# A fused attention and Fourier-mixing kernel: one batch's turn moved from DMA to TensorE, and the loads and scores around it reordered

## The chip, the cores and the metric

The kernel runs on one core of a Trainium2 chip. The metric is the device time of one execution in microseconds (us): 305.38 us before the change, the median of three runs (304.95 to 306.23). The profiled run has a span of 303.7 us from its first to its last instruction, at a mean granted TensorE clock of 0.994.

## The reference

Two models are chained. In the first, a sequence x of 512 tokens and a state of 32 rows attend to each other, for 8 batches and 8 heads of 64 columns:

```
scores  = x @ state^T / 8;   a  = softmax(scores);   xread = a  @ state
scores2 = state @ x^T / 8;   a2 = softmax(scores2);  sread = a2 @ x
u0 = concat(xread, sread)            # 544 rows of 512 columns per batch
```

In the second, the 544 x 512 result of each batch is mixed by a Fourier transform over rows and columns, normalised, and passed through a two-layer network:

```
u  = u0 + real(fft(fft(u0, rows), columns))
un = (u - mean) / sqrt(var + 1e-6)
out = u + relu(un @ w_ch1) @ w_ch2   # 512 -> 2048 -> 512
```

The matrix products run in bf16 with sums in float32.

## The kernel before

**Stages of one batch.** `attend(b)` turns the batch's x (512 x 512, in the bf16 tile `xin`) and its state block into `xT` and `sT`, so that columns of heads lie on partitions. Two `scores` steps multiply them (PSUM tile `esp`, L437) and ScalarE takes the exponential (tile `E`, L442); for batches from 2 on, `turn_scores` turns E on TensorE (tile `eTp`, L449) and ScalarE copies it to `ET` (L450). `xread` (L462, tiles `xrp` and `xfp`) and `sread_by_head` (L482) read the values; VectorE divides by the sums (L470, L471, L489) into the row tiles XF and XR. `fold` on VectorE (L534 to L549) adds and subtracts mirrored rows and columns, so that the transform needs only a quarter of the products; `read_low`, `fold_low` and `fold_low_again` do the same for 32 "low" rows on GpSimd (L519 to L531).

`transform(b)` does the Fourier transform as two sets of matmuls: `over_s` along the rows (L783, PSUM tile `gp`, copied to G by ScalarE, L784), `over_d` along the columns (L679 and L680, tile `yp`). VectorE adds the input (tile U, L684), takes the statistics (L337, L339), and centres (tile `ub`); `turn_u` turns the result into `unT`, on TensorE (L851, with a copy at L852) for batches 0 and 1, by DMA (L847) for the later ones. Two tiny GpSimd instructions per row tile form the inverse deviation (L343, L344; in the first batches these "roots" are collected and issued later).

`layer1(b)` has 16 steps of four 128 x 512 matmuls (L926; for batch 0 quarter steps of 128 columns, L936), each with a relu on ScalarE (L928, L938). `layer2(b)` has 16 steps of four matmuls (L990, tile `po`); each fourth ends with `store`, in which VectorE adds U (tile `ot`, L957) and SyncE stores it. The lists are called L and M for batch 0: M[0] to M[3] are the four quarters of the first row tile, M[4] to M[7] of the second. M[0] and M[4] use the first quarter of the second weights `w2`, M[1] and M[5] the second, and so on.

**What sets the order.** Every engine runs its instructions in the order in which the program records them. The opening and all of batch 0 and 1 up to L1224 are a list written by hand; from batch 1's layers on (L1226 to L1250), `weave` merges streams of steps: a stream is given with two numbers between 0 and 1, the stretch of the round over which its steps are spread.

**Buffers.** The PSUM pools are `psQ` (three tiles, tag q: gp, yp, eTp, tp and others), `psF` (three tiles, tag c: ph, po and the warm-up) and `psX` (one double tile, tag x). `xs`, the float32 landing place of x, has two buffers; `xin` has two as well.

**The names that the change touches.** `x_by_dma` (L355) is the first batch whose x and state are turned by DMA on SyncE's queue (L377 for sT, L388 for xT) and not on TensorE. `turn_all` (L400) turns x and the state of one batch on TensorE, 16 + 4 transposes, and leaves three copies in a list: sT and half of xT on ScalarE, the other half on VectorE. Before, batch 1 alone uses it. `load_x(b)` issues seven DMAs for one batch's x (L145), `turn_in_dram` reverses a batch's state rows from DRAM to DRAM (L155), `load_state` loads them (L113). `second_weights(lo, hi)` issues quarters of w2 on GpSimd's queue (L325); in front of it stands a `gate`, a tiny GpSimd copy that reads x of batch 2 and so holds the weight loads until that x has landed. `cast_columns` casts x of batch 2 to bf16 on GpSimd; the last four columns are cast behind another gate, which reads the last quarter of w2 (L1174), so that the DMA turns of batch 2 start only when the weights have landed:

```
    nc.gpsimd.tensor_copy(gate, w2[:, 12:16, 0])
    cast_columns(508, 512, slice(0, 4))
    turned[2]()
    load_x(3)
```

Of the kernel before, what the change touches and what calls it, by code (L numbers as in the profile page):

```python
# [30 lines left out]
def kernel(  # L31
# [8 lines left out]
    nc = tc.nc  # L40
    B, H, S, D = x.shape
# [67 lines left out]
    def states(lo, hi):  # L109
        return stf[:, lo:hi] if lo < 3 else stl[:, lo - 3:hi - 3]  # L110

    def load_state(lo, hi, src=state):
        nc.sync.dma_start(  # L113
            out=states(lo, hi).rearrange("p b g d -> p (b g) d"),
            in_=src[lo:hi].rearrange("b (g hh) j d -> (hh j) (b g) d", hh=4),
        )

    xin_bufs = [singles.tile([128, 4, 514], BF16, name=f"xin{i}") for i in range(2)]
    xs_of = {}
# [34 lines left out]
    def turn_in_dram(lo, hi):  # L154
        nc.sync.dma_start(out=s_dram[lo:hi].rearrange("b h j d -> (b h) j d"),  # L155
                          in_=state[lo:hi, :, ::-1, :].rearrange("b h j d -> (b h) j d"))
# [19 lines left out]
    gate = singles.tile([128, 4], F32, name="gate")  # L176
# [9 lines left out]
    w2 = singles.tile([128, FC, dm], BF16, name="w2")  # L186
# [136 lines left out]
    def second_weights(lo, hi):  # L323
        for q in range(lo, hi):
            nc.gpsimd.dma_start(out=w2[:, q * 4:(q + 1) * 4, :], in_=w2v[:, q * 4:(q + 1) * 4, :])  # L325
# [3 lines left out]
    def qt(name, dt=F32):  # L329
        return psQ.tile([128, 512 if dt == F32 else 1024], dt, name=name, tag="q")  # L330
# [21 lines left out]
    first_roots = []  # L352


    x_by_dma, u_by_dma = 2, 2  # L355


    turned = {}

    def attend(b):  # L360
# [24 lines left out]
        def turn_x(g):  # L385
            if b >= x_by_dma:
                for si in ((0, 1), (3, 2))[g]:
                    nc.sync.dma_start_transpose(out=xT[:, :, 128 * si:128 * si + 128], in_=xin[:, si, 1:513])  # L388
                return
            p = qt("xTp", BF16)  # L390
            for si in range(2):
                for pr in range(4):
                    o = si * 512 + pr * 128
                    nc.tensor.transpose(p[:, o:o + 128], xin[:, 2 * g + si, 1 + 128 * pr:129 + 128 * pr], ident)
            (nc.vector.tensor_copy if g == (b == 0) else nc.scalar.copy)(
                xT[:, :, 256 * g:256 * g + 256].rearrange("p a (s c) -> p s a c", c=128),
                p.rearrange("p (s a c) -> p s a c", s=2, c=128))
# [15 lines left out]
        copies, pairs = [], []  # L413
# [137 lines left out]
        if b < 2:  # L551
            first = [turn_state, lambda: turn_x(0), lambda: turn_x(1)]
            if b == 1:
                first = [turn_all] + [lambda i=i: copies[i]() for i in range(3)]
            first += [lambda: scores_t(0), lambda: scores_t(1),
                     lambda: scores(0), lambda: scores(1)]
        else:
            first = [lambda: scores(0), lambda: scores(1), lambda: turn_scores(1), lambda: turn_scores(0)]
            if b >= x_by_dma:
                turned[b] = lambda: (b > 2 and turn_state(), turn_x(0), turn_x(1))  # L560
                turned[b, 0] = turn_state
            else:
                first = [turn_state, lambda: turn_x(0), lambda: turn_x(1)] + first
        read = lambda c0, rev, o: lambda: xread(c0, rev, "xrp" if rev else "xfp", o, apart=(b == 0 and not rev))
        if b < 2:
            second = [read_low, fold_low, fold_low_again, read(0, False, XF[:, 0, 0:512]), sread_heads,
# [347 lines left out]
    def layer1(key):  # L914
        low = isinstance(key, tuple)
        n = 128 if low else 512
        hT = wk.tile([128, FC, n], BF16, name="hTL" if low else "hT", tag="hTL" if low else "hT", bufs=1 if low else 2)
        h_of[key] = hT
        per = 512 // n

        def step(i):
            ph = psF.tile([128, 512], F32, name="ph", tag="c")
            for f in range(per * i, per * i + per):
                o = (f % per) * n
                for c in range(DC):
                    nc.tensor.matmul(ph[:, o:o + n], lhsT=w1[:, c, f * 128:(f + 1) * 128], rhs=un_of[key][:, c, :],  # L926
                                     start=(c == 0), stop=(c == DC - 1))
            nc.scalar.activation(hT[:, per * i:per * i + per, :].rearrange("p a b -> p (a b)"), ph, AF.Relu,  # L928
                                 scale=-1.0 / 512 if key == 0 else -1.0 if key in flipped else 1.0)

        def quarter_step(i, r):
            ph = psF.tile([128, 512], F32, name="ph", tag="c")
            for f in range(4 * i, 4 * i + 4):
                o = 128 * (f % 4)
                for c in range(DC):
                    nc.tensor.matmul(ph[:, o:o + 128], lhsT=w1[:, c, f * 128:(f + 1) * 128],  # L936
                                     rhs=un_of[key][:, c, 128 * r:128 * r + 128], start=(c == 0), stop=(c == DC - 1))
            nc.scalar.activation(hT[:, 4 * i:4 * i + 4, 128 * r:128 * r + 128], ph.rearrange("p (a b) -> p a b", b=128),  # L938
                                 AF.Relu, scale=-1.0 / 512 if key == 0 else -1.0 if key in flipped else 1.0)

        if key == 0:
            return [lambda i=i, r=r: quarter_step(i, r) for r in range(4) for i in range(FC // 4)]
        return [lambda i=i: step(i) for i in range(FC // per)]
# [80 lines left out]
    turn_state, turn_x0, score, read, sread, state_rows, even, odd = open_batch()  # L1024
    begin, terms_of, low_of, out_of, keep_low, over_d, add_sums, centre_sums, turn_u, spread, done, keep_middle = transform(0)
# [83 lines left out]
    psF = ctx.enter_context(tc.tile_pool(name="psF", bufs=3, space=bass.MemoryType.PSUM))  # L1109
    pool_of = {"warm": (psF, "c")}  # L1110
    s1, r1 = attend(1)
    scores_next, reads_after = attend(2)
    L, M = layer1(0), layer2(0)
    over_s1, over_d1, add1, centre1, turn_u1, done1 = transform(1)
    turns1, copies1, s1 = s1[0], s1[1:4], s1[4:]
    def cast_columns(lo, hi, i):
        nc.gpsimd.tensor_copy(xin_bufs[0][:, i, 1 + lo:1 + hi], xs_of[2].rearrange("p (i c) -> p i c", i=4)[:, i, lo:hi])
# [13 lines left out]
    nc.gpsimd.tensor_tensor(gate, xs_of[0][:, 0:4], w1[:, :, 3 * 512], op=ALU.add)  # L1131
    load_x(2)
    turn_in_dram(3, 4)
    turned[2, 0]()
    load_state(3, 4, s_dram)
    turn_u(0, 1)
    add_sums(0, 0)
    centre_sums(0, 0)
# [12 lines left out]
    L[2]()  # L1151
    s1[2]()
    r1[0]()
    nc.gpsimd.tensor_copy(gate, xs_of[2].rearrange("p (i c) -> p i c", i=4)[:, :, 0])
    second_weights(0, 2)
    r1[1]()
    r1[2]()
    second_weights(2, 4)
    L[3]()
    s1[3]()  # L1160
    r1[3]()
# [7 lines left out]
    r1[7]()  # L1169
    nc.gpsimd.tensor_copy(gate, XQs[1].rearrange("p (g j c) -> p g j c", g=2, j=4)[:, 1, 3, 0:4])  # L1170
    for i in range(4):
        cast_columns(0, 508, slice(i, i + 1))
    state_blocks(3, 4, nc.gpsimd.tensor_copy)
    nc.gpsimd.tensor_copy(gate, w2[:, 12:16, 0])  # L1174
    cast_columns(508, 512, slice(0, 4))
    turned[2]()
    load_x(3)
    turn_in_dram(4, B)
    L[6]()
    L[7]()  # L1180
    turn_u(1, 0)
    spread(0, 1)
    state_ones(2, B)
    L[8]()
# [29 lines left out]
    turn_u1(1, 1)  # L1214
    M[6]()
    turn_u1(1, 0)
    spread(0, 0)
    spread(1, 1)
    spread(1, 0)
# [5 lines left out]
    l2, scores_first = M, scores_next  # L1225
    for b in range(1, B + 1):  # L1226
        reads_next = reads_after
        l2, l2_now = (layer2(b), [l2[7]] + l2[8:]) if b == 1 else (layer2(b) if b < B else [], l2)
        streams = [(l2_now + (layer2(("L", b // 4)) if b in (3, 7) else []), 0, 1)]
        if b == 1:  # L1230
            streams = [(l2_now[:5], 0, 0.38), (l2_now[5:], 0.6, 1)]
        if b < B:
            streams.append((layer1(b), 0.13 if b == 2 else 0.08, 1))
        if b + 1 < B:
            if b == 1:
                streams.append(([lambda: load_state(4, B, s_dram), lambda: state_blocks(4, B, nc.gpsimd.tensor_copy)], 0.2, 0.95))
                streams.append((scores_first[0:2], 0, 0.08))
                streams.append((scores_first[2:4], 0.08, 0.15))
            streams.append((reads_next, 0.17 if b == 1 else 0, 0.42 if b == 1 else 0.3))
            streams.append((transform(b + 1), 0.58 if b == 1 else 0.47, 0.88 if b == 1 else 0.85))  # L1240
        if b + 2 < B:
            scores_next, reads_after = attend(b + 2)
            streams.append(([lambda: (cast_x(b + 2), turned[b + 2]())], 0.15 if b == 1 else 0.2, 0.2))
            streams.append((scores_next, 0.5, 1))
        if b + 3 < B:
            streams.append(([lambda: load_x(b + 3)], 0.35, 0.35))
        if b in (3, 7):
            streams.append((low_rows(b // 4), 0.02, 0.2))
            streams.append((layer1(("L", b // 4)), 0.36, 0.8))
        weave(*streams)  # L1250
# [30 lines left out]
```

The softmax here doesn't subtract the row's maximum and nothing guards it: scores larger than these inputs give would overflow.

## Time and profile before

| engine | busy us | share of the span |
|---|---|---|
| TensorE, matmuls (PE) | 288.9 | 95% |
| TensorE, weight loads (PEld, beside PE) | 165.3 | 54% |
| VectorE (DVE) | 180.4 | 59% |
| ScalarE (ACT) | 136.3 | 45% |
| GpSimd (POOL) | 92.7 | 31% |

SyncE (SP) issues most DMAs and computes nothing. A busy share is a mean over the whole span; where time can be saved is read from the slices of the span, from the waits of the busiest engine, and from the timeline at those places. In the timeline the columns are the start, the busy time, engine, line, operation and tiles, and in brackets how long the engine had been idle before it and for whom.

Some times that are needed below, all from the trace: TensorE begins the quarter steps of batch 0's first layer at 22.3 us, M[0] at 38.3 and the weave (M[7]) at about 52. Batch 2's x is issued at 21.3 to 28.3 us and batch 3's at 52.1 to 57.2. The four quarters of w2 are issued at 31.5, 32.3, 38.2 and 39.0 us and take 5.4 to 8.3 us to land.

### The profile page before, as it was taken

To read this page: it belongs to the slowest core of one execution; us is meant where nothing else is said; L and a number is where in the kernel's file an instruction comes from. 1 tells how busy PE (TensorE), PEld (TensorE's weight loads), DVE (VectorE), ACT (ScalarE), POOL (GpSimd) and SP (SyncE) were. 2 spreads that over 40 slices of the span, in tenths; PEclk is the share of its full clock that TensorE was granted. 3 is DMA by queue.
4 is the path that set the end of the run, shared out by engine and by line. 5 is a ranking of instruction groups with operands and counts; after the bars stand their busy time and mean duration, and the time that the engine had idled before them with its cause. 6 is when DMAs were issued, how large, how long until landed. Compare 5 with 4: busy or idle time off the path is not lost.

```text
span 303.7 us, 6027 instructions
## 1 busy us (share of the span) xinstructions
PE 288.9 (95%) x2301; PEld 165.3 (54%) x2333; DVE 180.4 (59%) x446; ACT 136.3 (45%) x253; POOL 92.7 (31%) x226
## 2 busy tenths in 40 slices
PE   5999989888999999999999999999999999999995
PEld 5789966434544645456545554455454544555443
DVE  8868987573879385755637575675668474000012
ACT  6887557434633553244533445254524442334200
POOL 6764862750481044301315022702240131000000
PEclk9999999997999999999999999999999999999999
DMA  8998793958533952467433684253243023600355
GB/s 155 197 204 185 129 175 73 209 110 179 113 86 72 207 131 78 107 144 167 96 80 72 148 164 89 69 123 82 74 90 69 37 75 86 133 2 35 87 128 132
DMA packets 110824, 34.86 MB, mean 115 GB/s; under 512 B 101980, under 2 KB 106332, under 8 KB 110796
## 3 DMA queue, kind: packets, MB, share of 16 engines
q1 hardware_dynamic: 100076, 28.72, 43.3%
q0 software_dynamic: 4224, 4.19, 8.6%
q10 hardware_dynamic: 6496, 1.57, 2.5%
q8 instruction: 18, 0.29, 0.4%
q14 instruction: 10, 0.08, 0.1%
HBM read 22.41 MB, written 14.02 MB: 120 GB/s over the span
## 4 chain that ended last, share of the span: by engine, by line
PE 76%; DMA 6%; DVE 5%; POOL 5%; SPq 4%; issue 3%; ACT 1%; POOLq 0%; DVEq 0%
PE po L990 33%; PE ph L926 32%; DMA w<-in_moe_w_ch_dram 2%; PE gp L783 2%; SPq L145 2%; DMA xT<-xin 2%; SPq L388 1%; DMA xs<-in_x_dram 1%; PE po L982 1%; PE esp L437 1%; PE yp L680 1%; PE yp L679 1%; PE xfp L462 1%; DVE U L684 1%; DVE st L337 1%
## 5 line engine op out<-in xcount | busy, mean ns | idle before, releaser
L990 PE MATMUL po<-w,hT 128*128 128x512 bf16 x480 | 122.2, 379 | 1.3 <-issue 0.5
L928 ACT ACTIVATE hT<-ph 128x512 bf16<-128x512 f32 x112 | 66.9, 597 | 121.0 <-PE ph L926 118.9
L926 PE MATMUL ph<-unT,w 128*128 128x512 bf16 x432 | 113.7, 382 | 0.7
L926 PEld LDWEIGHTS <-w 128*128 128x128 bf16 x576 | 50.9, 98 | 47.3 <-issue 1.1
L990 PEld LDWEIGHTS <-hT 128*128 128x128 bf16 x496 | 46.6, 98 | 46.0
L957 DVE SCALAR_TENSOR_TENSOR ot<-po,rstd,U 128x512 f32<-128x512 f32 (+2 forms) x33 | 24.1, 732 | 50.8 <-PE po L990 46.0
L787 POOL COPY GL<-G 128x128 bf16<-128x128 bf16 x7 | 2.0, 289 | 75.7 <-ACT G L784 75.7
L684 DVE TENSOR_TENSOR U<-yp,XR 128x512 f32<-128x512 f32 x14 | 9.6, 682 | 24.8 <-PE yp L680 24.8
L337 DVE BATCH_NORM_STATS2 st<-U 128x6 f32<-128x512 f32 x32 | 21.8, 682 | 0.1
L344 POOL TENSOR_TENSOR rstd<-rstd,mhalf 128x1 f32<-128x1 f32 x34 | 20.0, 587 | 2.7
L343 POOL TENSOR_TENSOR rstd<-mv,epst 128x1 f32<-128x1 f32 x34 | 6.6, 194 | 44.3 <-DVE mv L339 44.2
L936 PE MATMUL ph<-unT,w 128*128 128x128 bf16 x256 | 16.2, 219 | 0.5 <-DVE unT L852 0.3
L784 ACT CAST G<-gp 128x288 bf16<-128x288 f32 x28 | 13.2, 481 | 6.1 <-PE gp L783 6.1
L936 PEld LDWEIGHTS <-w 128*128 128x128 bf16 x256 | 15.0, 98 | 0.9 <-issue 0.8
L842 DVE TENSOR_SCALAR ub<-U,mv 128x512 bf16<-128x512 f32 x24 | 12.3, 511 | 0.9
L938 ACT ACTIVATE hT<-ph 128x512 bf16<-128x512 f32 x16 | 9.5, 596 | 6.8 <-PE ph L936 6.8
L148 POOL CAST xin<-xs 128x2048 bf16<-128x2048 f32 (+1 forms) x9 | 11.7, 1317 | 1.4 <-DMA xs<-in_x_dram 1.3
L519 POOL COPY XT<-XR 32x514 bf16<-32x514 bf16 x7 | 4.2, 603 | 22.4 <-DVE XR L471 22.4
L442 ACT ACTIVATE E<-esp 128x512 bf16<-128x512 f32 x14 | 8.4, 597 | 5.7 <-PE esp L437 5.7
L471 DVE TENSOR_TENSOR XR<-xrp,rs 128x512 bf16<-128x512 f32 x14 | 9.7, 695 | 0.5
L471 DVE TENSOR_TENSOR XF<-xfp,rs 128x512 bf16<-128x512 f32 x14 | 9.7, 692 | 0.5
L684 DVE TENSOR_TENSOR U<-yp,XF 128x510 f32<-128x510 f32 x14 | 9.4, 673 | 0.0
(245 smaller groups left out, 376.0 us busy)
## 6 DMA issues: line engine op xcount, KB each, us to landing
xs<-in_x_dram SPq DMA_DIRECT2D x22, 256.0 KB, 4.6
w<-in_moe_w_ch_dram POOLq DMA_DIRECT2D x8, 512.0 KB, 7.9
out_dram<-ot SPq DMA_DIRECT2D x15, 256.0 KB, 3.5
r_dram<-ot SPq DMA_DIRECT2D x14, 256.0 KB, 2.3
out_dram<-r_dram SPq DMA_DIRECT2D x14, 256.0 KB, 3.5
xs<-in_x_dram SPq DMA_DIRECT2D x8, 192.0 KB, 4.5
xs<-in_x_dram ACTq DMA_DIRECT2D x2, 256.0 KB
l_dram<-ot SPq DMA_DIRECT2D x2, 256.0 KB
```

Source lines behind the costliest of these rows:

```text
L148: copy(xin_bufs[b % 2][:, lo:hi, 1:513], xs_of[b].rearrange("p (i c) -> p i c", i=4)[:, lo:hi])
L337: nc.vector.bn_stats(st6, u)
L344: nc.gpsimd.tensor_tensor(rstd, rstd, mhalf, op=ALU.pow)
L471: nc.vector.tensor_tensor(ov, in0=p[ps, :, 0:256].rearrange("p g (h d) -> p g h d", d=D), in1=rs[ps].unsqueeze(3).to_broadcast([n, 2, 4, D ...
L684: nc.vector.tensor_add(u.rearrange("p (k r) -> p k r", r=2), p.rearrange("p (r k) -> p k r", r=2)[:, 0:u.shape[1] // 2, :], x.rearrange("p ...
L784: nc.scalar.copy(G[:, j, :].rearrange("p (i q) -> p q i", q=2), p[:, 0:NM].rearrange("p (q i) -> p q i", q=2))
L842: nc.vector.tensor_scalar(t, in0=ud, scalar1=mv[:, 0:1], scalar2=None, op0=ALU.subtract)
L926: nc.tensor.matmul(ph[:, o:o + n], lhsT=w1[:, c, f * 128:(f + 1) * 128], rhs=un_of[key][:, c, :], start=(c == 0), stop=(c == DC - 1))
L928: nc.scalar.activation(hT[:, per * i:per * i + per, :].rearrange("p a b -> p (a b)"), ph, AF.Relu, scale=-1.0 / 512 if key == 0 else -1.0 ...
L936: nc.tensor.matmul(ph[:, o:o + 128], lhsT=w1[:, c, f * 128:(f + 1) * 128], rhs=un_of[key][:, c, 128 * r:128 * r + 128], start=(c == 0), st ...
L957: nc.vector.scalar_tensor_tensor(ot[:, cols], in0=po_of[i][:, 0:cols.stop - cols.start], scalar=rstd, in1=u[:, cols], op0=ALU.mult, op1=AL ...
L990: nc.tensor.matmul(po_of[i], lhsT=h_of[key][:, f, i * 128:(i + 1) * 128], rhs=w2[:, f, :], start=(f == 0), stop=(f == FC - 1))
```

## The change

Batch 2 joins batch 1 in being turned on TensorE: its 20 transposes and three copies stand behind the last `turn_u1`, ahead of M[3]. With no DMA turns of batch 2 to wait for, `load_x(3)` and the next `turn_in_dram` move up to stand right behind batch 2's load, the cast of batch 2 needs no second part and no gate on w2, and SyncE's queue is freed of six DMA turns. On GpSimd the low-row fold of batch 1 (r1[1], r1[2]) comes ahead of the gate and of all four quarters of w2, where before it stood between the second quarter and the third. One copy of `turn_u(1, 0)` goes from VectorE to ScalarE. In the first round of the weave the scores of batch 2 start a little later (0.04 instead of 0), and so do its reads and its transform; the scores of batch 3 start at 0.66 of the round instead of 0.5.

```diff
-    x_by_dma, u_by_dma = 2, 2
+    x_by_dma, u_by_dma = 3, 2
...
-                first = [turn_state, lambda: turn_x(0), lambda: turn_x(1)] + first
+                first = [turn_all] + [lambda i=i: copies[i]() for i in range(3)] + first
...
     scores_next, reads_after = attend(2)
+    turns2, copies2, scores_next = scores_next[0], scores_next[1:4], scores_next[4:]
...
     load_x(2)
     turn_in_dram(3, 4)
-    turned[2, 0]()
     load_state(3, 4, s_dram)
+    load_x(3)
+    turn_in_dram(4, B)
...
     r1[0]()
-    nc.gpsimd.tensor_copy(gate, xs_of[2].rearrange("p (i c) -> p i c", i=4)[:, :, 0])
-    second_weights(0, 2)
     r1[1]()
     r1[2]()
-    second_weights(2, 4)
+    nc.gpsimd.tensor_copy(gate, xs_of[2].rearrange("p (i c) -> p i c", i=4)[:, :, 0])
+    second_weights(0, 4)
...
     for i in range(4):
-        cast_columns(0, 508, slice(i, i + 1))
+        cast_columns(0, 512, slice(i, i + 1))
     state_blocks(3, 4, nc.gpsimd.tensor_copy)
-    nc.gpsimd.tensor_copy(gate, w2[:, 12:16, 0])
-    cast_columns(508, 512, slice(0, 4))
-    turned[2]()
-    load_x(3)
-    turn_in_dram(4, B)
     L[6]()
     L[7]()
-    turn_u(1, 0)
+    turn_u(1, 0, nc.scalar.copy)
...
     turn_u1(1, 0)
+    turns2()
+    for c in copies2:
+        c()
...
-                streams.append((scores_first[0:2], 0, 0.08))
-                streams.append((scores_first[2:4], 0.08, 0.15))
-            streams.append((reads_next, 0.17 if b == 1 else 0, 0.42 if b == 1 else 0.3))
-            streams.append((transform(b + 1), 0.58 if b == 1 else 0.47, 0.88 if b == 1 else 0.85))
+                streams.append((scores_first[0:2], 0.04, 0.12))
+                streams.append((scores_first[2:4], 0.12, 0.2))
+            streams.append((reads_next, 0.22 if b == 1 else 0, 0.46 if b == 1 else 0.3))
+            streams.append((transform(b + 1), 0.62 if b == 1 else 0.47, 0.9 if b == 1 else 0.85))
...
-            streams.append((scores_next, 0.5, 1))
+            streams.append((scores_next, 0.66 if b == 1 else 0.5, 1))
```

## The prediction

> **What bounds the kernel now.** I read the page's busy shares, then its 40 slices, the list of what TensorE waited for, and TensorE's timeline where the slices dip.
>
> ```profile
> PE 288.9 (95%) x2301; PEld 165.3 (54%) x2333; DVE 180.4 (59%) x446; ACT 136.3 (45%) x253; POOL 92.7 (31%) x226
> PE   5999989888999999999999999999999999999995
> PEclk9999999997999999999999999999999999999999
> ```
>
> TensorE sets the time: only time saved on it counts. Behind the opening it has two soft places: slices 7 to 9 (some 46 to 76 us), and the one digit 7 of the clock. The waits name them:
>
> ```profile
> PE esp L437 <- DMA xT<-xin: 2.6, 3, 1.4
> PE gp L783 <- DVE unT L852: 1.0, 1, 1.0
> PE eTp L449 <- ACT E L442: 0.6, 1, 0.6
> ```
>
> ```profile
> 68.07 0.29 PE L437 MATMUL esp<-sT,xT 128*128 128x64 bf16 x4 [1.42 <-DMA xT<-xin]
> 69.40 0.29 PE L437 MATMUL esp<-sT,xT 128*128 128x64 bf16 x4 [1.04 <-DMA xT<-xin]
> 69.52 1.50 PE L926 MATMUL ph<-unT,w 128*128 128x512 bf16 x4
> ```
>
> The scores of batch 3 wait 1.42 + 1.04 us for x turned by DMA, and the four matmuls behind them take 1.50 us instead of 1.03. The windows tell why (columns: stretch, its length, busy us and count of PE, PEld, DVE, ACT, POOL, then granted clock, DMA share, GB/s):
>
> ```profile
> 65.00:70.00 5.00, 2.54 (x19) 1.10 (x18) 4.80 (x12) 1.74 (x4) 0.00 (x0) 0.99 0.43 88
> 70.00:75.00 5.00, 4.95 (x29) 2.94 (x29) 1.27 (x3) 2.79 (x6) 0.00 (x0) 0.66 0.83 190
> ```
>
> After the idle 2.5 us the granted clock is 0.66 over the next 5 us: 0.34 x 5 = 1.7 us more. The chain of waits gives the root, long before:
>
> ```profile
> 38.98 7.44 DMA w<-in_moe_w_ch_dram
> ...
> 46.54 0.19 POOL gate L1174
> ...
> 48.15 1.26 SPq L388
> 49.45 1.26 SPq L388
> 50.76 2.50 DMA xT<-xin
> ```
>
> Batch 2's DMA turns wait for the last quarter of the second weights (gate L1174) and run at 46.9 to 53.3 us; on the same SyncE queue load_x(3) comes only at 52.1, and batch 3's turns end at 69.4.
>
> To size it I count TensorE from 51.01 (M[3]) to 76.44 (end of batch 2's first yp group), 25.43 us. Work in it: 18 layer steps of four 128x512 at 0.864 = 15.55; 4 score halves at 0.225 = 0.90; 2 eTp groups 0.47; 4 reads 0.88; srp 0.36; gp 1.13; yp 0.43; in all 19.72. So **5.7 us** are idle or slow: 2.46 + 1.7 at batch 3's scores, 0.17 + 0.58 at batch 2's, the rest in small gaps.
>
> **What the skill says.** *TensorE: Matmul & The Clock Gate*, Part 1: an idle window of about 3.4 us halves the clock. The trace agrees in kind; here 2.5 us idle sufficed. *SBUF — State Buffer*, "SBUF: two separate sides": GpSimd and a VectorE op with two SBUF inputs exclude each other on a shared port pair. The trace agrees: the same low-row fold takes GpSimd 5.2 us beside VectorE's fold of batch 1, and 3.0 us for batch 2, beside reads from PSUM:
>
> ```profile
> 33.06 1.12 POOL L523 TENSOR_TENSOR XEl<-XT 32x256 f32<-32x256 bf16 x1
> 61.93 0.66 POOL L523 TENSOR_TENSOR XEl<-XT 32x256 f32<-32x256 bf16 x1
> ```
>
> *DMA: Bandwidth & Descriptors*, "Issuing engines are not separate DMA queues": the weight loads of GpSimd and SyncE's x loads share 16 engines. The trace shows w1 (issued 10.0 to 14.5) and batch 1's x together: landings up to 11.7 us, against 5.4 for a w2 quarter alone.
>
> **The change, part by part.**
>
> *1. Folds ahead of w2, all w2 behind one gate.* Before, w2's first quarter is issued at 31.52 and lands 6.2 later, at 37.7; M[0] takes it at 38.30. So it had 0.6 us to spare. After, GpSimd goes from XT's copy (ends 29.5) into the fold. VectorE then mostly reads PSUM, so I take 3.0 us rather than 5.2: end 32.5, the gate on x (x has landed, 30.9) to 32.7, 0.27 issue gap, first issue 32.95. Landing takes 6.2 (as before) to 7.1 (w1's first quarter, beside x); I take 6.6: **39.5**, with 39.1 and 42.2 (slow fold, 35.1 + 7.1) as ends. M[0] is ready at 38.0, so it stalls 1.5 us, and over_s1(2) and all of TensorE queue behind it. But before, over_s1(2) waited 1.0 us right behind M[0], for VectorE's copy of turn_u(1,0), and 0.17 ahead of it. The copy now goes to ScalarE (0.57 us, in its 0.3 us gaps between relus, and unT is wanted only at 42), and VectorE's fold, rid of its rival, ends 1.6 us earlier. M[0] then ends at 40.4, where over_s1(2) stood at 40.33: **net 0**. Quarters 2 to 4 follow at 0.77 us per issue and some 2.6 us of data each, so the last lands near 48; their first users stand at 44.9, 48.8 and 51.0: hidden.
>
> *2. load_x(3) behind load_x(2).* It issues at about 32 to 37 instead of 52 to 57. w2 will starve its tail, but cast_x(3) comes only at 59: hidden. Batch 3's turns leave a SyncE queue without load_x(3) in front: casts at 59 to 61, turns to 67.2, landing 69.6; the scores now stand at 73.9 on TensorE: hidden. The 2.46 and 1.7 us go. Without cost beside these: gate L1174 and the last four columns of the cast fall away (GpSimd, which then waits for stats anyway), the two sT turns leave SyncE at 29.1 to 31.8, so that load_state(3) is issued no later than before, and turn_in_dram(4, B) comes 20 us earlier into a queue that is empty till the first store at 56.
>
> *3. Batch 2's x turned on TensorE.* 20 transposes. The same group for batch 1 stands from 20.22 to 21.34:
>
> ```profile
> 20.22 1.06 PE L404 MATMUL xTp<-ident,xin 128*128 128x128 bf16 x16
> 21.11 0.39 PE L408 MATMUL sTp<-ident,stb 128*128 128x128 bf16 x4
> ```
>
> So **+1.12 us** from 51.0 on. Its copies (ScalarE 0.59 + 1.02, VectorE 0.68) lie beside M[3] and M[7] (1.73 us), so the scores at 54.0 don't wait. But VectorE's copy stands ahead of three stats pairs (0.81 each) and these ahead of ot(0), which frees one of three PSUM buffers: copy 52.2 to 52.85, stats to 55.27, ot to 55.97. M[8] wants the buffer at 55.3: **+0.7**.
>
> *4. The later scores.* From M[8] at 56.0 I count on: last read of batch 2 at 65.3, four layer-1 steps in a row to 68.95, then over_s(0). It needs VectorE's fold, behind srp's four multiplies (63.5 to 64.7), ot (0.75), two reads (0.9 each); the fold starts near 67.3, its first product comes 3.3 later, at 70.6: **+1.65**. over_s(2) waits **+0.4** more for L548 and batch 3's second eTp pair stands one step ahead of its reader: **+0.1**.
>
> *Sum:* -5.7 + 1.12 + 0.7 + 1.65 + 0.4 + 0.1 + 0 = **-1.7 us**. After that all moves together: yp and so batch 2's unT come about 2 us earlier too. 305.4 - 1.7 = **303.7**.
>
> **Rivals.** (a) *The second weights come late.* The fold keeps its 5.2 us or descriptors wait: first issue 35.1, landing 41.7 or later, M[0] stalls 3.7 us, 2.2 more than taken, and so long a gap brings the slow clock back (1.7): -1.7 + 2.2 + 1.7 = +2.2, **307.6**, slower. For it: w2 had only 0.6 us to spare. Against: batch 2's fold at 3.0 us. (b) *VectorE is quick enough:* stalls of part 3 and 4 mostly vanish (small idle gaps of VectorE take them up): -1.7 - 2.0, **301.7**. For it: before, VectorE idled 2.43 us ahead of its first read (57.8), so the queue has room. (c) *The slow clock moves* to the gap at over_s(0) (1.65 + 0.4 idle within 3.4 us): **305.4**, no change. Against: at 38.0 to 40.3, 1.2 us idle did not bring it; 2.5 did.
>
> **Numbers.** Forecast 0.5: my terms are good to some 1 us, and the 0.5% line stands at 303.85, so 0.3 of it is faster and 0.2 the same. (a) 0.18, slower; (b) 0.2, faster; (c) 0.12, the same. Together: faster 0.5, same 0.3, slower 0.2. The range leaves out the far ends of (a) and (b): 301.6 to 307.0.
>
> **What would show it.** Right: GpSimd's L523 near 29.5 at 0.6 to 0.7 us and the first w2 issue near 33; M[0] near 39.5 waiting for the w2 DMA while no unT wait follows; no xT wait at the esp groups; clock near 1.0 at 70 to 75; a wait of over_s(0) for VectorE's XQ of 1 to 2 us; M[8] waiting for ot. Wrong if w2's first quarter lands past 41, if the clock falls between 38 and 46, or if TensorE waits for xT of batch 3 again.

## The result: slower, by a stall at the first second-layer step and by copies that waited for each other

| | us, median (lowest to highest) | ratio to before, 95% interval | span of the profiled run |
|---|---|---|---|
| before | 305.27 (304.95 to 306.23) | | 303.7 |
| after | 310.33 (309.13 to 311.08) | 1.0157 (1.0115 to 1.0199) | 308.1 |

The change makes the kernel 1.6% slower. The forecast was 303.7 us and its range ended at 307.0, so both the direction and the range were wrong. What happened is what rival (a) describes, second weights that come late and a slow clock behind them, but not by its route: the fold was quick, as forecast, and it was the transfer that took long. The rest of the change lost time too, where every case but (c) had counted on a gain.

The page of the kernel after, the same three lines as shown of before (busy shares, TensorE's busy tenths in 40 slices of 7.7 us, granted clock):

```profile
PE 290.0 (94%) x2321; PEld 165.5 (54%) x2353; DVE 179.4 (58%) x446; ACT 138.4 (45%) x256; POOL 90.7 (29%) x224
PE   5999969797999999999999999999999999999995
PEclk9999979999999999999999999999999999999999
```

The twenty added matmuls are the new transposes. Slice 5 (38.5 to 46.2 us; slices are counted from 0) has a 6 where before had an 8, and it also has the clock's one digit 7, which stood in slice 9 before. Slices 7 and 9 are still soft. TensorE's waits behind the opening, longest first (engine, line, what it waited for: us in total, times, longest):

```profile
PE po L990 <- DMA w<-in_moe_w_ch_dram: 3.2, 1, 3.2
...
PE xrp L462 <- DVE XF L471: 0.9, 1, 0.9
PE gp L783 <- DVE XQ L543: 0.9, 1, 0.9
...
PE po L990 <- ACT hT L928: 0.7, 1, 0.7
PE esp L437 <- ACT E L442: 0.7, 1, 0.7
PE esp L437 <- DVE xT L411: 0.6, 1, 0.6
```

The waits of esp for xT by DMA and of gp for unT, which stood in the list of before, are gone. In their place stands one long wait for w2, and five of 0.6 to 0.9 us. The chain of waits of after, asked for 30 to 42 us (start, length, what), shows where the long one comes from:

```profile
32.15 0.37 POOL XQl L531
32.52 0.08 POOL gate L1158
32.60 8.49 DMA w<-in_moe_w_ch_dram
41.09 0.05 issue
41.14 0.60 PE po L990
```

The low-row fold ends at 32.5, the gate opens and the first quarter of w2 is issued at 32.60. That is within 0.4 us of the prediction, which had 32.5 and 32.95. But the quarter takes **8.49 us** to land, against 6.2 before. On SyncE's timeline batch 3's x is issued in the same stretch, from 1.2 us before that on:

```profile
31.41 6.81 SPq L145 DMA_DIRECT2D xs<-in_x_dram  x7
```

The windows (stretch, its length, busy us and count of PE, PEld, DVE, ACT, POOL, then granted clock, DMA share, GB/s) show what the idle time did to the clock:

```profile
40.00:45.00 5.00, 3.64 (x17) 2.20 (x19) 0.00 (x0) 0.96 (x2) 2.13 (x7) 0.66 1.22 196
65.00:70.00 5.00, 4.84 (x57) 2.56 (x57) 3.21 (x10) 1.79 (x3) 4.80 (x9) 1.00 0.56 118
70.00:75.00 5.00, 4.06 (x21) 1.69 (x19) 4.34 (x9) 2.31 (x4) 0.01 (x1) 1.00 0.45 93
```

At 65 to 75 us, where before lost 1.7 us to the slow clock, the clock is now full. The same loss, 0.34 x 5 = 1.7 us, stands at 40 to 45 instead. Before has the loss in most of its executions and not in all: of its 71 beside experiments 4, 5, 7 and 8, 47 had a mean granted clock under 0.997 and a median of 305.89 us, the other 24 a median of 304.42.

**Where the 4.4 us of span went.** I cut the span at three marks that both kernels have: the last `tp` product of batch 1, right ahead of M[3] (50.79 before, 54.15 after), batch 3's first read (84.26 and 88.59), and the end.

| stretch | before | after | difference | forecast |
|---|---|---|---|---|
| start to the last `tp` of batch 1 | 50.79 | 54.15 | +3.36 | 0 |
| to batch 3's first read | 33.47 | 34.44 | +0.97 | -1.7 |
| to the end | 219.4 | 219.5 | +0.1 | 0 |

The first difference adds up. M[0] starts 2.84 later (41.14 against 38.30). The wait of gp for unT behind it vanishes: from M[0] to that gp it takes 2.03 us in before (38.30 to 40.33) and 0.87 in experiment 8 below, where nothing is waited for, so 1.16 are saved. The slow clock costs 1.66 (experiment 2 below). Together that is +3.34. The second difference is split further down.

### The profile page after: what moved, and what is told of

It reads as the page before. It is cut to its first block, busy times and chain, and to the rows that moved or that the text cites. A ratio compares the mean times of both kernels' runs of the same rounds, so it can differ in the third digit from the quotient of the medians.

```text
span 308.1 us, 6064 instructions
## 1 busy us (share of the span) xinstructions
PE 290.0 (94%) x2321; PEld 165.5 (54%) x2353; DVE 179.4 (58%) x446; ACT 138.4 (45%) x256; POOL 90.7 (29%) x224
## 3 DMA queue, kind: packets, MB, share of 16 engines
q10 hardware_dynamic: 6496, 1.57, 2.5%
## 4 chain that ended last, share of the span: by engine, by line
PE 77%; DMA 9%; DVE 6%; POOL 2%; SPq 2%; ACT 2%; issue 1%; ACTq 0%; POOLq 0%; DVEq 0%
PE po L990 35%; PE ph L926 31%; DMA s_dram<-in_state_dram 3%; DMA w<-in_moe_w_ch_dram 3%; PE gp L783 2%; DMA xs<-in_x_dram 2%; SPq L145 2%; DMA gen<-s_dram 1%; PE ph L936 1%; PE po L982 1%; PE yp L680 1%; PE esp L437 1%; PE yp L679 1%; PE xrp L462 1%; PE xfp L462 1%
## 5 line engine op out<-in xcount | busy, mean ns | idle before, releaser
L928 ACT ACTIVATE hT<-ph 128x512 bf16<-128x512 f32 x112 | 66.9, 597 | 119.7 <-PE ph L926 117.6
L926 PE MATMUL ph<-unT,w 128*128 128x512 bf16 x431 | 112.3, 379 | 0.8
```

## The experiments

Each ratio is to the kernel before, run on the same chip beside it. Times of runs from different chips are compared only through these ratios.

**1. The first two quarters of w2 back ahead of the fold, all else as in after.**

```diff
+    nc.gpsimd.tensor_copy(gate, xs_of[2].rearrange("p (i c) -> p i c", i=4)[:, :, 0])
+    second_weights(0, 2)
     r1[1]()
     r1[2]()
-    nc.gpsimd.tensor_copy(gate, xs_of[2].rearrange("p (i c) -> p i c", i=4)[:, :, 0])
-    second_weights(0, 4)
+    second_weights(2, 4)
```

> The changed kernel with one part undone: the gate on x and the first two quarters of the second weights stand again ahead of the low-row fold (first issue near 31.5 us instead of 32.6), the other two behind it; batch 3's x is still loaded at about 31 to 38 us. Theory 1 (the x load beside it stretches the weights' landing): the first quarter takes about 8 us as in the changed kernel (8.5) and lands at 39.5 to 40; M[0] waits 1.5 to 2 us, the slow clock may stay away; 1.5 to 3 us less than the changed kernel's 310.3. Theory 2 (the issue 1.1 us later is what was lost): landing 6.2 us after the issue, at 37.7, no wait at M[0], some 4.5 us less, 306.

Measured: 306.18 us, ratio 1.0022 (1.0008 to 1.0037), span 303.9. The first quarter is issued at 31.22, 0.25 us ahead of batch 3's x, and takes 7.1 us: it is in at 38.3. M[0] in TensorE's timeline waits for nothing:

```profile
38.52 0.81 PE L990 MATMUL po<-w,hT 128*128 128x512 bf16 x2
```

Neither theory holds as it was written. The x load did stretch the landing, but to 7.1 and not to 8, and M[0] does not wait, as theory 2 had it.

**2. Batch 3's x loaded some 10 us later, the fold first as in after.**

```diff
     load_state(3, 4, s_dram)
-    load_x(3)
-    turn_in_dram(4, B)
...
     state_blocks(3, 4, nc.gpsimd.tensor_copy)
+    nc.gpsimd.tensor_tensor(gate, xs_of[0][:, 0:4], w2[:, 12:16, 0], op=ALU.add)
+    load_x(3)
+    turn_in_dram(4, B)
```

> The changed kernel with batch 3's x load held on GpSimd until the last quarter of the second weights has landed, as it came to stand in the kernel before; the fold stays ahead of the weights. Theory 1 (contention of the x load): the first quarter lands 6.2 to 6.6 us after its issue at 32.6, at 38.8 to 39.2, M[0] waits about 1 us instead of 3.2, no slow clock at 40 to 45: 3.5 to 4.5 us less than the changed kernel, 306 to 307. Theory 2 (late issue): landing stays near 41, no gain, 310.

The new gate was meant to hold x until the last quarter of w2 has landed. The trace shows that it does not: SyncE issues x from 41.14 us on, after 9.3 us of waiting that the profile puts down to GpSimd's cast of batch 2's x, while the gate runs at 47.94. But at 41.14 the first quarter is in, and that is what the comparison needs.

Measured: 305.43 us, ratio 1.0006 (0.9987 to 1.0026), span 303.3, as theory 1 has it and a little better. M[0] in the timeline, and the window where after had 0.66:

```profile
38.40 0.82 PE L990 MATMUL po<-w,hT 128*128 128x512 bf16 x2 [0.25 <-DMA w<-in_moe_w_ch_dram]
```

```profile
40.00:45.00 5.00, 4.70 (x55) 3.55 (x54) 3.54 (x10) 2.75 (x6) 2.20 (x7) 1.00 1.18 182
```

The two runs with the two originals make a square. Each cell has when the first quarter of w2 was issued, how long it took, and when it was in:

| | batch 3's x not under way | batch 3's x beside it |
|---|---|---|
| w2 ahead of the fold | before: 31.52 + 6.2 = 37.7 | experiment 1: 31.22 + 7.1 = 38.3 |
| w2 behind the fold | experiment 2: 32.87 + 5.5 = 38.4 | after: 32.60 + 8.5 = 41.1 |

M[0] is ready at about 38.2 (37.9 to 38.5). Either move alone uses up the slack of 0.6 us and little more: no wait in experiment 1, and 0.25 us in experiment 2. Both together stall TensorE by 3.20 us, and the stall brings the slow clock. The two moves don't just add: 7.1 + 5.5 - 6.2 would give a landing of 6.4 us, and 8.5 was measured. Each landing is that of one profiled run, and the cell of before is the kernel before as a whole; that corner was not run inside the changed kernel. From experiment 2 to after, the first transpose of batch 2 moves from 49.97 to 54.37: 4.40 us, of which 2.74 is M[0]'s later start and the other 1.66 is the clock. In experiment 2 x of batch 3 is issued from 41.1 to 50.8 us instead of 31.4 to 38.2, and TensorE still waits for no xT of batch 3: the early load bought nothing.

**3. The turned x of batch 2 in two PSUM tiles, all else as in after.** In after, ScalarE's copy (L410) and VectorE's (L411) read two halves of one PSUM tile. VectorE's timeline of after (in brackets the idle time ahead, and what ended it) shows what became of the second:

```profile
57.22 0.69 DVE L411 COPY xT<-xTp 128x1024 bf16<-128x1024 bf16 x1 [2.22 <-ACT xT L410]
```

The transposes end at 55.4, and yet VectorE stands idle until ScalarE's copy is done.

```diff
+            other = qt("xTq", BF16) if b == 2 else t[:, 1]
...
-                    nc.tensor.transpose(t[:, pr // 2, 512 * (pr % 2) + ...
+                    nc.tensor.transpose((other if pr > 1 else t[:, 0])[:, 512 * (pr % 2) + ...
...
-            copies.append(lambda: nc.vector.tensor_copy(xT[:, 2:4, :], t[:, 1].rearrange(...)))
+            copies.append(lambda: nc.vector.tensor_copy(xT[:, 2:4, :], other.rearrange(...)))
```

> The changed kernel, with the two halves of batch 2's turned x in two PSUM tiles, so that VectorE's copy (L411) no longer waits for ScalarE's copy (L410) of the same tile. Theory 3 (the two copies one behind the other cost TensorE the wait at the scores and put VectorE's statistics and first store back by 1.9 us): the 0.6 us wait at the first score half shrinks to 0 to 0.2, ot comes 1.5 us earlier, 1 to 2 us less than 310.3. Rival: the same time is lost at the next limit (second score half waiting for the first exponential, VectorE's fold): under 0.5 us.

Measured: 307.34 us, ratio 1.0040 (1.0012 to 1.0069), span 305.6. From the first transpose to batch 3's first read it takes 32.83 us (53.59 to 86.42), against 34.22 in after: 1.39 less, as theory 3 has it. Of the rest of the 2.5 us in span 0.8 is M[0]'s earlier start: w2's first quarter took 7.6 us here instead of 8.5. The slow clock came all the same (L783 starts every 0.12 us behind M[0]):

```profile
40.35 0.50 PE L991 MATMUL po<-w,hT 128*128 128x512 bf16 x1 [2.31 <-DMA w<-in_moe_w_ch_dram]
```

**4. Both 2 and 3.** 

> The changed kernel with both faults taken away: batch 3's x held until the second weights have landed (305.4 alone) and the two copies of batch 2's turned x from two PSUM tiles. If the two effects add: 1.4 us less than with the first alone (what the copies gave between the turns and batch 3's first read), 304.0. Rival: hidden behind VectorE's fold, 305.4.

Measured: 304.00 us, ratio 0.9959 (0.9939 to 0.9979), span 302.1. This is the changed kernel without its two faults, and it is 0.4% faster than before. The two effects add, as expected. M[0] still waits 0.5 us for w2. Against experiment 2 it gains 0.47% in the ratios, 1.4 us, and the same stretch takes 32.82 us against 34.22. VectorE's copy now comes right behind the transposes (line numbers are one higher here):

```profile
51.24 0.69 DVE L412 COPY xT<-xTq 128x1024 bf16<-128x1024 bf16 x1 [0.47 <-PE xTq L405]
```

**5. As 4, with the scores, reads and transform of batch 2 at their places from before** (scores 0 to 0.08 and 0.08 to 0.15, reads 0.17 to 0.42, transform 0.58 to 0.88).

> The same as the run before it, with the first round's streams put back where the kernel before had them, all but batch 3's scores: batch 2's scores from 0, reads from 0.17, its transform from 0.58. Theory 5 (the later reads and transform bring TensorE to over_s before VectorE's fold is done, 0.9 us, and to a read that waits 0.9 us for the PSUM tile of the one before): these waits shrink to under 0.5 us together, some 1 us less than the run before it, 303. Rival: the reads then wait for the exponentials and the turned scores, no gain, 304.

Measured: 304.55 us, ratio 0.9984 (0.9958 to 1.0009), span 302.0. No gain over 4: the waits changed names only (0.7 for ScalarE's copy of xT, 0.6 for E, 1.8 at `over_s(0)` instead of 0.9). So no cost of the later places of batch 2's steps shows.

**6. The kernel before, with the scores of batch 3 at 0.66, and nothing else.**

```diff
-            streams.append((scores_next, 0.5, 1))
+            streams.append((scores_next, 0.66 if b == 1 else 0.5, 1))
```

> The kernel before, with one part of the change alone: in batch 1's round the scores of batch 3 start at 0.66 instead of 0.5. Theory 4 (the 2.5 us wait for batch 3's turned x and the 1.7 us of slow clock are a matter of where the scores stand, and no load has to move): both vanish, 2.5 to 4 us less than 305.3, 301.3 to 303. Rival: VectorE's fold of batch 2 or batch 3's later steps take their place and the time stays within 1 us of 305.3.

Measured: 303.24 us, ratio 0.9922 (0.9893 to 0.9950), span 301.1. The DMA turns of batch 3 are issued up to 69.4 us, as before, but the scores now stand at 73.5 and find them done. The two windows in which before had 0.99 and 0.66:

```profile
65.00:70.00 5.00, 3.23 (x21) 1.49 (x19) 4.84 (x11) 2.38 (x6) 0.00 (x0) 1.00 0.44 90
70.00:75.00 5.00, 4.83 (x40) 2.89 (x40) 2.24 (x5) 3.21 (x7) 0.29 (x1) 1.00 0.84 191
```

One new wait comes, 1.8 us at `over_s(0)` for VectorE's fold. The clock stays at 1.00 behind it. So this one number removes the xT wait and the slow clock, which the moved loads were meant to remove.

**7. As 6, with the copy of `turn_u(1, 0)` on ScalarE.** 

> The kernel before with two parts of the change: batch 3's scores from 0.66 of the round on, and the copy of turn_u(1, 0) on ScalarE. Against the late scores alone (303.2) the 0.8 us wait of over_s(2) for VectorE's copy falls away. If TensorE's order is all that counts: 0.8 less, 302.4. Rival: batch 2's DMA turns, which wait for the last quarter of the second weights, don't come earlier, so TensorE waits that much longer at batch 2's scores: 303.2, no gain.

Measured: 303.29 us, ratio 0.9934 (0.9916 to 0.9951), span 301.4, as the rival has it. The copy's wait at `over_s1(2)` goes and M[4] starts 0.8 us earlier (40.20 against 40.99), but then the scores of batch 2 wait 0.58 us for xT by DMA, which they did not do in 6. No gain: the DMA turns of batch 2 are a second limit right behind the first.

**8. As 7, with the fold ahead of w2.** 

> The same with the low-row fold ahead of the gate and of all four quarters of the second weights, as in the change; batch 2 still turned by DMA and batch 3's x loaded behind that, so nothing is loaded beside the weights. Theory 1 (contention made the weights late): the first quarter lands 5.5 to 6.2 us after its issue near 32.6, M[0] waits 0.2 to 0.9 us, no slow clock, M[4] stands near 39.9 instead of 40.95; 302 to 302.6. Theory 2 (the fold in front is itself the fault): M[0] waits over 2 us, 304 or more. The same rival at batch 2's scores as above: 303.2.

Measured: 303.80 us, ratio 0.9973 (0.9946 to 1.0000), span 302.2. Without x of batch 3 beside it the first quarter lands in 5.7 us, and M[0] waits 0.4. The gate on the last quarter of w2 runs at 46.80 instead of 46.21, the DMA turns of batch 2 start as much later, and its scores wait 1.46:

```profile
PE esp L437 <- DMA xT<-xin: 1.5, 1, 1.5
...
PE po L990 <- DMA w<-in_moe_w_ch_dram: 0.4, 1, 0.4
```

Theory 1 holds for the landing, and the rival for the time: the fold ahead of w2 pays nothing in the kernel before, where the turns hang on w2.

**9 and 10. As 7, with the transform of batch 2 at 0.62 to 0.9, and the scores of batch 3 from 0.66 (9) or 0.6 (10).**

> The kernel before with three parts of the change: batch 3's scores from 0.66, the copy of turn_u(1, 0) on ScalarE, and batch 2's transform at 0.62 to 0.9, which puts a fourth layer-1 step in front of over_s(0), where TensorE waits 1.8 us for VectorE's fold without it. If the step fills the wait: 0.9 us less than act_late (303.3), 302.4. Rival: later gp and yp groups put batch 2's turned result back and TensorE waits for it at batch 2's first layer: 303.3 or more.

> The same with batch 3's scores from 0.6, so that the first half of them also stands between the first gp group and the others, near 70.5 us, 1 us behind the landing of batch 3's turned x (69.4). If TensorE then fills the wait for XQ of the second half: 0.2 us less again, 302.2. Rival: the scores meet the DMA turn again: a wait for xT of up to 1 us, 303.

Measured: 302.41 us, ratio 0.9928 (0.9899 to 0.9956), span 300.3, and 302.62 us, ratio 0.9937 (0.9907 to 0.9966), span 300.8. The wait at `over_s(0)` is halved; the waits of 9:

```profile
PE gp L783 <- DVE XQ L543: 1.4, 2, 0.9
```

The 302.4 expected of 9 came out to the tenth, but in the ratios it is no gain over 7 that the intervals show: before was faster on this chip too (305.06 against 305.71). In 10 the first scores of batch 3 stand at 70.25 and wait for nothing, so its rival did not come, but no gain shows either. Both kernels are faster than before and after. They are not told apart from experiment 6 or from each other by these intervals. Experiment 6 is the simplest of them: one number.

## Why the prediction was wrong, point by point

**Part 1, the fold and w2 (forecast 0, measured +3.36).** The fold was right to a tenth: L523 at 29.46 with 0.73 us, end 32.5, first issue 32.60 against 32.95. The two waits of gp did vanish. The step that failed is "Landing takes 6.2 (as before) to 7.1 (w1's first quarter, beside x); I take 6.6". It took 8.5, outside my own two ends, so M[0] stalled 3.20 us where the sum had 1.5, and "net 0" fell with it. The upper end came from w1's first quarter. That one too was issued behind a running x, as the timelines of before for SyncE and GpSimd show:

```profile
6.96 4.92 SPq L145 DMA_DIRECT2D xs<-in_x_dram  x7
9.97 2.45 POOL L310 DMA_DIRECT2D w<-in_moe_w_ch_dram  x3
```

What differs is how far x had come. From the rates in the DMA windows I estimate 0.5 of its 1 MB moved when w1 was issued, and 0.1 MB when w2 was (31.41 for x, 32.60 for w2). So w1's quarter may have met half an x and w2's a whole one; that this is the reason was not tried. The Trainium skill, *DMA: Bandwidth & Descriptors*, "Queues, rings and completion order", says that a DMA engine goes in turn through the queues that it has work for, a packet at a time; the landings agree in kind, since the same quarter takes 5.5 to 6.4 us without x and 7.1 to 8.5 beside it. My upper end of 42.2 held the landing at 41.1, but only by way of a slow fold, and only as an end of a range: the sum had no slow clock for it.

The slow clock (1.66 us) is the second half of the miss. Rival (a) named both and gave 307.6, though it had the weights late by a late issue (35.1), which did not come. That its landing of 41.7 is near the 41.1 measured is luck. Two of my three signs of being wrong came true: the landing past 41, and the fall of the clock between 38 and 46. The Trainium skill, *TensorE: Matmul & The Clock Gate*, Part 1, has an idle window of about 3.4 us that halves the clock; here 3.20 us idle brought it, and in experiment 3 it came after 2.31, so less than that window was enough.

The slices of before were misread as well. The soft ones were said to be 7 to 9, "some 46 to 76 us", but those are 53 to 76 us, and slice 5 (38 to 46 us) has an 8 too. That is where M[0] stands and where the change lost most.

**Part 2, x of batch 3 early.** "w2 will starve its tail ... hidden" looked at one direction only: that x slows w2 had no term in this part. The rest held: no xT wait of batch 3, full clock at 65 to 75. But experiments 2 and 6 show that the scores' later place was enough for that.

**The middle stretch (forecast -1.7, measured +0.97).** Let the work of this stretch be what TensorE is busy between the same two marks in experiment 6 (50.83 to 81.80), where the clock is full: 28.29 us.

| | before | after |
|---|---|---|
| work | 28.29 | 28.29 |
| slow clock (busy 30.05 less 28.29) | 1.76 | 0 |
| transposes and the like (29.86 less 28.29) | 0 | 1.57 |
| idle | 3.42 | 4.58 |
| sum | 33.47 | 34.44 |

1. *"So 5.7 us are idle or slow"* was too large. There were 1.76 + 3.42 = 5.18 in the whole stretch. I had counted each matmul at its ideal length, so that 0.52 of work stood as a gap to be won.
2. *Transposes +1.12*: 1.57 with what else differs. From 54.37 to the start of the next matmuls at 55.49 it is just 1.12.
3. *"so the scores at 54.0 don't wait"* was the step that failed most. It took the copies as independent. VectorE's copy waited for ScalarE's, and three waits stand on TensorE, here in its timeline:

```profile
57.97 0.39 PE L437 MATMUL esp<-sT,xT 128*128 128x64 bf16 x8 [0.59 <-DVE xT L411]
59.04 0.39 PE L437 MATMUL esp<-sT,xT 128*128 128x64 bf16 x8 [0.69 <-ACT E L442]
60.98 1.02 PE L990 MATMUL po<-w,hT 128*128 128x512 bf16 x4 [0.69 <-ACT hT L928]
```

   With two tiles the first and the last vanish, the middle one stays at 0.85, and the stretch is 1.4 us shorter. In the trace of before there was no sign of it: batch 1's two copies don't overlap there either (ScalarE 22.07 to 23.09, VectorE from 23.64), but VectorE had other work until then.

   *"M[8] wants the buffer at 55.3: +0.7"* measured 0.69. The list puts this wait (the last of the three) down to a relu on ScalarE (L928), but M[8] does not need that relu: in experiment 4 it starts before it (TensorE, ScalarE, VectorE):

```profile
55.37 1.03 PE L991 MATMUL po<-w,hT 128*128 128x512 bf16 x4
55.57 0.60 ACT L929 ACTIVATE hT<-ph 128x512 bf16<-128x512 f32 x1 [0.27 <-PE ph L927]
54.26 1.40 DVE L958 SCALAR_TENSOR_TENSOR ot<-po,rstd,U 128x512 f32<-128x512 f32 x2
```

   What fits in all runs is `ot`, as forecast: in after the first of the two ends at 60.97, and M[8] starts at 60.98; in experiment 4 it ends at 55.0, before M[8] comes. The size is luck: counted from the transposes, both `ot` and M[8] came 1.6 us later than forecast.
4. *over_s(0) +1.65* measured 0.91, *over_s(2) +0.4* measured 0.21, and *eTp +0.1* did not show. VectorE was quicker than I had it, in part as rival (b) said.
5. Not foreseen at all: a read waits 0.94 us for VectorE's division of the read before it, as both use the one double tile of `psX`:

```profile
71.46 0.40 PE L462 MATMUL xrp<-stb,ET 128*128 128x260 bf16 x2 [0.94 <-DVE XF L471]
```

   It also stands in experiment 4, in which no copy waits for another, so it belongs to the new spacing of the steps. In experiment 5, where the old places are back, no read waits in this way.

The idle time of after in this stretch is thus 1.81 from terms that I had (0.69 + 0.91 + 0.21) against 2.85 forecast, and 2.77 from terms that I had not: 0.59 + 0.69 + 0.94, and 0.55 of small ones. The four errors add up to the miss: 0.52 + 0.45 - 1.04 + 2.77 = 2.70.

**What stays open.** Why the landing is stretched by so different amounts. The lead of x over w2 was -0.25, 0.87 and 1.19 us in experiment 1, experiment 3 and after, with landings of 7.1, 7.6 and 8.5; but w1's first quarter, with a lead of 3.0 us, took 7.1. So the lead alone does not set the price. A landing with x started at other distances from w2 was not tried.

## What to carry to other kernels

Before moving a load earlier, look for the tightest load that will be in flight beside it, and price that one with more than one landing: beside an x load a quarter of the weights took from 7.1 to 8.5 us here, and the one case on hand was at the low end. Two moves that use the same half microsecond of slack can each be free and together not. A stall of TensorE can cost more than its length: here 3.20 us of it cost 1.66 more in clock. Before moving any load for a wait, try to let the waiting step come later: here that one number gave a gain of 0.8%, and no other version tried is shown to be faster.

## What was new on the hardware

- The first quarter of w2 landed in 5.5 to 6.4 us in the nine profiled runs with no x load beside it, and in 7.1, 7.6 and 8.5 us in the three with one.
- The slow clock shows in the spacing of single products: L783 starts every 0.12 us at 42.8 to 43.9 in after, against 0.06 in before at 40.3 to 40.9. It came behind 2.31 us of idle time (experiment 3), behind 3.20 (after) and behind 1.42 + 1.04 with a short group between them (before), and not behind 1.8 (experiment 6).
- Two engines' copies out of the halves of one PSUM tile ran one behind the other (2.22 us of VectorE idle time); out of two tiles they ran side by side. The trace shows the wait; whether the chip or the program's order demands it was not tried apart.
